# A gated mix of linear attention and a GLU on one core: the last stage's products, its addition of b, and how M is read

## The chip, the cores and the metric

The kernel runs on one core of a Trainium2 chip. The metric is the device time of one execution in microseconds (us); lower is better. TensorE multiplies into PSUM, VectorE and ScalarE work on SBUF and PSUM, and DMAs are issued here from two queues, SyncE's (SP) and GpSimd's (POOL).

## The reference

```python
H = 32; Dh = D // H                      # x: 2048 x 640
q, k, v = split_heads(x @ wqkv)
phi = lambda t: jnp.where(t > 0, t + 1, jnp.exp(t)) + 1e-6
kv = jnp.einsum("bhsd,bhse->bhde", phi(k), v)
z = jnp.einsum("bhsd->bhd", phi(k))
num = jnp.einsum("bhqd,bhde->bhqe", phi(q), kv)
den = jnp.einsum("bhqd,bhd->bhq", phi(q), z)[..., None] + 1e-6
a = merge_heads(num / den) @ wo
b = (_sigmoid(x @ w_gate) * (x @ w_up)) @ w_down     # F = 1536
g = _sigmoid((x * gate_w).sum(-1, keepdims=True))
return g * a + (1 - g) * b
```

Everything is fp32. The kernel uses that kv then wo is one matrix for all tokens: with M the 640 x 640 matrix of kv (32 blocks on a diagonal) times wo, and with P the phi(q) of a token scaled by g/den, g * a is P M. So the last stage is one product of 640 x 640 by 640 x 2048, to which (1 - g) * b is added.

## The kernel before

An fp32 product is made of three matmuls on halves: `split` (L245) takes the rounded half `hi` of an operand on ScalarE (`act`, L228) and the rest `lo` on VectorE (`vec2`, L232), and `mm3` (L215 to 218) multiplies hi by hi, hi by lo and lo by hi into the same PSUM tile. In the traces lines 216 to 218 are therefore nearly all of TensorE's work. A helper, `vec3`, stands at L236.

The tokens are four groups g of TG = 512, the 640 features KC = 5 rows u, k or o of 128. The output is kept transposed, so that one output tile is rows o of 128 features by 512 tokens of a group g: 5 x 4 = 20 tiles. A tile takes 5 terms k of 3 matmuls, 15 matmuls of 128x128 by 128x512. PSUM has four tags, `rot`, `dd`, `cc` and `ch`, of two buffers each.

Stages that matter here, in their order in time:
- Early on (DMAs of 163.6 to 188.4 us), `m_part` (L1227) writes M to `m_dram`, 120 rows at a time.
- The first pass of the GLU and of q, for groups 2 and 3 (`f_phase(1, ...)`), writes b of these groups to `b_dram`. At its step (3, 7) it calls `m_rows` (L1359): four DMAs on POOL's queue that copy `m_dram` to `mr_dram` with its rows permuted, so that a row of 128 partitions holds what phi(q)'s transposed rows need.
- The second pass, for groups 0 and 1 (`f_phase(0, ...)`), starts `queue_m` at its step (2, 7): a fifth u of `mr_dram` is loaded on SP's queue into the tile `mr`, split into the tile `mt`, written to `mp_dram` from POOL's queue, and then the next fifth is started. b of groups 0 and 1 is summed up in the SBUF tile `tb`; `last_down` (L1757) makes its last twenty sums, every second one by a DMA on POOL's queue that accumulates (`ds` to `tb`).
- Near the end of that pass the halves of M are loaded back from `mp_dram` (`load_m`, into tiles of the names `ws` and `wf`), and P of the groups from `p_dram` (`load_p`), where phi(q) had been put.

The names `ws`, `wu`, `wg` are tiles for the weights' forms in the GLU: each f of its blocks loads one of each on SP's queue (`load_form`, L901 to 903). The GLU's `Block` (L988) makes the four outputs of a 2 x 2 partition in seven products in place of eight, s1 to s7, with sums of operands and of outputs.

The last stage (the loop over `groups` = (2, 3, 0, 1)) makes the 20 tiles one after the other, here called units and numbered from 0. For each group it queues the scaling of its five b rows by 1 - g (`scale_b`, into the same tile `bl` or `tb`), first in the queue and from row 4 to row 0; then, for the next group, the scaling of P (`pq_scale`, L1882: plus EPS, times `fac`) and its split (`queue_pq`). After a unit `finish` (L1905) adds the PSUM tile to the scaled b row and sends it to the output. `load_b` loads 1 - g (`omg`) and b: for group 2 five DMAs, rows 4 to 0 (L1872), for group 3 two of three and two rows (L1876, L1877). The last unit is made in halves of 256 tokens.

The order of instructions on the engines is fixed by the program, not by a scheduler of the compiler. The class `Order` keeps a model of how far TensorE, ScalarE and VectorE have come, and queues of items with their costs. After each product `fill` issues the items whose end, by the model, is not more than some slack behind TensorE; an item can have a time before which it isn't taken (`ready`), `first=True` puts it before all others, `spare=True` behind them; `need(key)` issues all items up to that key at once. What stands in an engine's queue is done in that order, whatever arrives first. The lines that issue nothing but DMAs run where the Python runs them.

## Time and profile before

| | |
|---|---|
| median of three runs | 754.36 us (754.12 to 755.03) |
| the profiled execution's own time | 753.48 us |
| its span in the trace | 751.8 us |
| mean granted clock of TensorE | 0.999 |

The span is what the trace covers, from the first to the last instruction; the execution's own time has 1.68 us more around it. The busy time by stretches of the span:

```
us, PE busy (x) PEld busy (x) DVE busy (x) ACT busy (x) POOL busy (x), PEclk, DMA share, GB/s
330.00:520.00 190.00, 190.00 (x855) 157.83 (x855) 139.47 (x238) 83.49 (x148) 26.14 (x45) 1.00 0.69 249
520.00:606.00 86.00, 84.89 (x374) 69.94 (x373) 67.11 (x115) 28.84 (x51) 2.14 (x4) 1.00 0.66 243
606.00:679.00 73.00, 73.00 (x323) 60.39 (x323) 55.65 (x86) 20.37 (x36) 4.00 (x5) 1.00 0.54 187
679.00:751.80 72.80, 69.00 (x317) 56.95 (x315) 43.48 (x73) 9.72 (x16) 0.85 (x1) 0.99 0.51 172
```

PE is TensorE's matmuls, PEld its loads of weights, DVE VectorE, ACT ScalarE, POOL GpSimd; the DMA share is the mean busy share of the core's 16 DMA engines. The last stretch is the last stage. Matmuls are pipelined: the distance between the starts of two of them is their cost, and their own durations overlap. Some records of matmuls are missing from a trace (a few in a hundred), so that TensorE's line may show a hole that isn't one. A group of rows names its tiles as "out<-in"; the part in brackets is the idle time of the engine before the row, and what ended it.

### The profile page before, as it was taken

Reading aid. Unit: us, or ns where it says so; the run is one execution under the profiler, and the core shown is the slowest. Engines: PE = TensorE matmul, PEld = TensorE weight load, DVE = VectorE, ACT = ScalarE, POOL = GpSimd, SP = SyncE. Lnnn points to the kernel's source line nnn. Section 1 sums busy time; section 2 is a strip of 40 time slices with the busy share of each in tenths; the row PEclk is TensorE's granted clock in tenths of the full one; section 3 lists DMA queues with packets and bytes.
Section 4 is the critical chain, followed back from the end, with each engine's and each line's share of the span. In section 5 each row is a group of like instructions: output and inputs, shape, how many; then the busy total and the mean of one; then the engine's idle time right before and its main releaser. Section 6 shows DMA issues by size and latency. Waiting matters only on the chain.

```text
span 751.8 us, 10052 instructions
## 1 busy us (share of the span) xinstructions
PE 745.6 (99%) x3678; PEld 640.1 (85%) x3678; DVE 546.6 (73%) x964; ACT 316.9 (42%) x596; POOL 95.6 (13%) x153
## 2 busy tenths in 40 slices
PE   9999999999999999999999999999999999999998
PEld 8999999988888888888888888888788888888786
DVE  4877576867577768887878875576778876885854
ACT  5663537257555634343444354354223323222110
POOL 0210101012213422121211211000000000010000
PEclk9999999999999999999999999999999999999999
DMA  7563627686988888596675656967575656279333
GB/s 258 153 161 75 157 39 177 191 265 212 344 323 284 282 283 335 172 381 227 233 245 216 244 202 229 379 222 264 205 273 210 222 176 241 96 260 330 117 129 123
DMA packets 62758, 167.92 MB, mean 223 GB/s; under 512 B 9774, under 2 KB 23614, under 8 KB 59381
## 3 DMA queue, kind: packets, MB, share of 16 engines
q1 hardware_dynamic: 45941, 103.01, 40.9%
q0 software_dynamic: 16624, 64.10, 24.6%
q8 instruction: 29, 0.48, 0.3%
q10 hardware_dynamic: 144, 0.16, 0.1%
q14 instruction: 20, 0.16, 0.1%
HBM read 99.56 MB, written 62.78 MB: 216 GB/s over the span
## 4 chain that ended last, share of the span: by engine, by line
PE 93%; DMA 5%; DVE 1%; issue 0%; SPq 0%
PE ch L216 9%; PE ch L217 9%; PE ch L218 9%; PE dd L217 8%; PE dd L218 8%; PE dd L216 8%; PE rot L216 7%; PE rot L217 7%; PE rot L218 7%; PE cc L216 6%; PE cc L217 6%; PE cc L218 6%; DMA pl<-p_dram 2%; DMA ws<-wf 2%; DMA bl<-b_dram 1%; PE ch L1216 1%
## 5 line engine op out<-in xcount | busy, mean ns | idle before, releaser
L228 ACT ACTIVATE c<-ch 128x512 f32<-128x512 f32 x75 | 44.8, 597 | 161.4 <-PE ch L218 159.7
L232 DVE TENSOR_TENSOR hf<-c,hf 128x512 fp32r<-128x512 f32 x63 | 43.2, 688 | 30.2 <-ACT hf L228 29.7
L232 DVE TENSOR_TENSOR tb<-dd,tb 128x512 f32<-128x512 f32 x75 | 51.0, 687 | 12.1 <-PE dd L218 12.0
L232 DVE TENSOR_TENSOR c<-cc,c 128x512 f32<-128x512 f32 x50 | 34.4, 687 | 25.5 <-ACT c L228 19.5
L228 ACT ACTIVATE c<-c 128x512 f32<-128x512 f32 x48 | 30.2, 628 | 49.7 <-DVE c L232 49.6
L228 ACT ACTIVATE hf<-c 128x512 fp32r<-128x512 f32 x63 | 39.3, 625 | 18.4 <-DVE c L232 18.1
L232 DVE TENSOR_TENSOR tb<-rot,tb 128x512 f32<-128x512 f32 x59 | 40.0, 686 | 5.3 <-PE rot L218 5.2
L216 PE MATMUL ch<-xth,ws 128*128 128x512 f32 x100 | 39.0, 390 | 1.1 <-DMA ws<-wf 1.1
L218 PE MATMUL ch<-xth,ws 128*128 128x512 f32 x100 | 38.9, 389 | 0.0
L217 PE MATMUL ch<-xtl,ws 128*128 128x512 f32 x100 | 38.9, 389 | 0.0
L216 PE MATMUL dd<-xrh,wg 128*128 128x512 f32 x99 | 38.7, 391 | 0.0
L218 PE MATMUL dd<-xrh,wg 128*128 128x512 f32 x99 | 38.6, 390 | 0.0
L217 PE MATMUL dd<-xrl,wg 128*128 128x512 f32 x99 | 38.6, 390 | 0.0
L217 PE MATMUL rot<-pkl,xnh 128*128 128x320 f32 x102 | 31.5, 309 | 0.0
L218 PE MATMUL rot<-pkh,xnl 128*128 128x320 f32 x102 | 31.4, 308 | 0.0
L216 PE MATMUL rot<-pkh,xnh 128*128 128x320 f32 x102 | 31.4, 308 | 0.0
L232 DVE TENSOR_TENSOR c<-c,c 128x512 f32<-128x512 f32 x44 | 30.2, 686 | 1.3 <-ACT c L228 0.9
L216 PE MATMUL cc<-xbh,ws 128*128 128x512 f32 x75 | 29.2, 389 | 0.0
L217 PE MATMUL cc<-xbl,ws 128*128 128x512 f32 x75 | 29.2, 389 | 0.0
L218 PE MATMUL cc<-xbh,ws 128*128 128x512 f32 x75 | 29.2, 389 | 0.0
L216 PEld LDWEIGHTS ch<-xth,ws 128*128 128x128 f32 x100 | 18.8, 188 | 5.4 <-issue 1.5
L216 PE MATMUL dd<-hf,wd 128*128 128x512 f32 x60 | 23.3, 389 | 0.0
(482 smaller groups left out, 2286.4 us busy)
## 6 DMA issues: line engine op xcount, KB each, us to landing
wf<-ws POOLq DMA_DIRECT2D x12, 1152.0 KB, 6.5
ws<-wf SPq DMA_DIRECT2D x12, 1152.0 KB, 9.1
wst<-wst_f SPq DMA_DIRECT2D x12, 640.0 KB, 4.8
wf<-wg POOLq DMA_DIRECT2D x12, 640.0 KB, 5.3
wd<-wd POOLq DMA_DIRECT2D x12, 640.0 KB, 6.2
wg<-wf SPq DMA_DIRECT2D x12, 640.0 KB, 5.9
xst<-xt SPq DMA_DIRECT2D x10, 640.0 KB, 6.3
wf<-wd SPq DMA_DIRECT2D x10, 640.0 KB, 5.7
```

Of the source, the lines that this page charges most:

```text
L216: nc.tensor.matmul(out, l_hi, r_hi, start=first, stop=False, skip_group_check=True)
L217: nc.tensor.matmul(out, l_hi, r_lo, start=False, stop=False, skip_group_check=True)
L218: nc.tensor.matmul(out, l_lo, r_hi, start=False, stop=last, skip_group_check=True)
L228: nc.scalar.activation(out, src, fn, **kw)
L232: nc.vector.tensor_tensor(out, a, b, op=op)
L1216: nc.tensor.matmul(ps[:w, :w], v[:, m, :w], gt[:, m, c0:c0 + w], start=(m == 0), stop=(m == KC - 1))
```

## The change

There are three parts.

*The last stage.* P of group 1 is loaded before the stage's loop, right behind group 0's; b of groups 0 and 1 and the new loads of M behind the second unit. Groups 2 and 3 are made in units as before, and so are row 4 of group 0 and of group 1. Rows 0 to 3 of groups 0 and 1 are made in two blocks (`ABlock(0)`: rows 0 and 1, `ABlock(1)`: rows 2 and 3), each of which makes four tiles by seven products s1 to s7 of 2, 3, 2, 3, 2, 3 and 3 terms (s1, s2, s3, s4, s5, s7, s6 in the order of issue). For them `load_ms` reads two column pairs of M from `m_dram` again, by 16 DMAs on POOL's queue with pieces of 128 numbers, `queue_ms` makes the sums of M's blocks and splits them, and `queue_pt` the sums of P's blocks of groups 0 and 1.

*Gated b in PSUM.* The first three units scale b in SBUF and add it as before. For each later unit of groups 2 and 3, for row 4 of group 0, and for the s2 products, VectorE writes b times 1 - g into the PSUM tile before the products (`seed_b`), and the products are summed onto it; three units ahead, as an item that goes first. After such a unit ScalarE copies the tile to SBUF and the output is sent from there.

*M in permuted order.* `mr_dram` and its four DMAs are gone. `queue_m` reads the permuted rows straight from `m_dram`, by four DMAs of 32 rows on SP's queue for each fifth in place of one, and its item may be taken 14 us of the model after that, before 9.

```diff
-    mr_dram = dram.tile([P, KC, D], F32, name="mr_dram")
...
-    def m_rows():
+    def m_rows(dst, cols, queue, u=None):
 
         for d in range(4):
-            nc.gpsimd.dma_start(mr_dram[d * H:(d + 1) * H], m_dram.rearrange("(h u d) n -> d h u n", u=KC, d=4)[d])
+            m = m_dram.rearrange("(h u d) n -> d h u n", u=KC, d=4)[d]
+            queue.dma_start(dst[d * H:(d + 1) * H], m[:, u] if cols is None else m[:, :, cols])
 
     def queue_m(u=0):
 
         raw = down_pool[1].tile([P, D], F32, name="mr", tag="mr")
-        nc.sync.dma_start(raw, mr_dram[:, u])
-        at = max(order.pe, order.vec) + 9.0
+        m_rows(raw, None, nc.sync, u)
+        at = max(order.pe, order.vec) + 14.0
 
...
-        (3, 7): [m_rows],
...
-            PL[g] = []
+            PL[g], PL[g, "t"] = [], []
-                t = (x2_tile if n % 2 else h_tile)(dt=F32)
+                t = (x2_tile if n == 1 else h_tile)(dt=F32)
+                PL[g, "t"].append(t)
+        BL[g, "at"] = order.pe + 6.0
...
+    PT, MS, MR = {}, {}, {}
+    def load_ms(i):
+        if i == 0:
+            t = f32(down_pool[1].tile([P, 2, D], F32R, name="mt", tag="mt"))
+            raw = [t[:, j] for j in range(2)]
+        else:
+            raw = [down_pool[1].tile([P, D], F32, name=n, tag=n) for n in ("mr", "mv")]
+        for j in range(2):
+            c0 = (2 * i + j) * P
+            m_rows(raw[j].rearrange("p (k c) -> p k c", c=P), slice(c0, c0 + P), nc.gpsimd)
+        MR[i] = raw, order.pe + 9.0
+    def queue_ms(i):
+        raw, at = MR.pop(i)
+        w = 2 * P
+        g, v = raw
+        a11, a12, a21, a22 = g[:, :w], g[:, w:2 * w], v[:, :w], v[:, w:2 * w]
+        g5, v5 = g[:, 2 * w:], v[:, 2 * w:]
+        def sums(part):
+            if part == 0:
+                add(a22, a21, a22)
+                sub(a21, a11, a21)
+            else:
+                sub(a11, a22, a11)
+                sub(a12, a12, a11)
+                sub(g5, g5, v5)
+        def form(n, src):
+            if i not in MS:
+                t = ws_tile() if i == 0 else None
+                MS[i] = [t[:, c] for c in range(2)] if t is not None else \
+                    [wg_tile().rearrange("p a b -> p (a b)")[:, :9 * P] for _ in range(2)]
+            h, l = (t[:, n * w:n * w + width(src)] for t in MS[i])
+            split(h, l, src)
+        for part in range(2):
+            order.add(0, 2 * v_cost(w), lambda part=part: sums(part), None, lambda: at)
+        for n, t in enumerate((a22, a11, a21, a12, g5)):
+            order.add(a_cost(width(t)), v_cost(width(t)), lambda n=n, t=t: form(n, t), ("ms", i))
+    def queue_pt():
+        (b11, b21, _), (b12, b22, _) = PL[0, "t"], PL[1, "t"]
+        T = (b11, b22, b12, b21)
+        w = 2 * TG
+        def form(t):
+            if t == 1:
+                f = [[down_pool[2].tile([P, TG], F32R, name="pt", tag="c2", bufs=4) for _ in range(2)]
+                     for _ in range(2)]
+                PT[t] = f
+                for j in range(2):
+                    split(*f[j], T[t][:, j])
+                return
+            f = [x2_tile("pt", F32R) if t == 0 else x3_tile("pt", F32R) for _ in range(2)]
+            PT[t] = [[u[:, j] for u in f] for j in range(2)]
+            split(f[0][:, 0:2], f[1][:, 0:2], T[t])
+        def queue(t):
+            order.add(a_cost(w), v_cost(w), lambda: form(t), ("pt", t))
+        for a, b, c in ((b11, b12, b11), (b12, b22, b12), (b22, b22, b11), (b21, b21, b22)):
+            order.add(0, v_cost(w), lambda a=a, b=b, c=c: sub(a, b, c))
+        queue(1)
+        return queue
...
-    for gi, g in enumerate(groups):
-        for u in range(KC):
-            order.need(("pq", g, u))
-        for o in reversed(range(KC)):
-            order.add(0, v_cost(TG), lambda o=o: scale_b(g, o), ("b", g, o), first=True)
-        if 0 < gi < NG - 1:
-            nxt = groups[gi + 1]
-            queue_scale(nxt)
-            pq_tiles(nxt)
-            queue_pq(nxt)
-        for o in range(KC):
-            os_ = slice(o * P, (o + 1) * P)
-            cuts = (0, TG // 2, TG) if gi == NG - 1 and o == KC - 1 else (0, TG)
-            for c0, c1 in zip(cuts, cuts[1:]):
-                ps = ps_tile(("rot", "dd", "cc", "ch")[(o + gi) % 4])
-                prod(ps[:, c0:c1], [(MHL[k, 0][:, os_], MHL[k, 1][:, os_], PQ[g][k][0][:, c0:c1],
-                                     PQ[g][k][1][:, c0:c1]) for k in range(KC)], True)
-                order.need(("b", g, o))
-                finish(g, o, ps, c0, c1)
-            order.fill()
-        if gi == 1:
-            load_p(groups[3])
+    load_p(groups[3])
+    SEED = {}
+    def seed_b(g, o, tag):
+        SEED[g, o] = ps = ps_tile(tag)
+        vec2(ps, BL[g][o], OMG[g], OP.mult)
+    def queue_seed(g, o, tag, first=True):
+        order.add(0, v_cost(TG), lambda: seed_b(g, o, tag), ("b", g, o), lambda: BL[g, "at"], first=first)
+    def a_unit(g, o, cuts=(0, TG), tag="rot", seed=False):
+        os_ = slice(o * P, (o + 1) * P)
+        if seed:
+            order.need(("b", g, o))
+        for c0, c1 in zip(cuts, cuts[1:]):
+            ps = SEED.pop((g, o)) if seed else ps_tile(tag)
+            prod(ps[:, c0:c1], [(MHL[k, 0][:, os_], MHL[k, 1][:, os_], PQ[g][k][0][:, c0:c1],
+                                 PQ[g][k][1][:, c0:c1]) for k in range(KC)], not seed)
+            if seed:
+                dst = BL[g][o]
+                act(dst, ps, AF.Copy, "p")
+                nc.sync.dma_start(out_t[o * P:(o + 1) * P, g * TG:(g + 1) * TG], dst)
+                continue
+            order.need(("b", g, o))
+            finish(g, o, ps, c0, c1)
+    def queue_b_scale(g, os_):
+        for o in os_:
+            order.add(0, v_cost(TG), lambda o=o: scale_b(g, o), ("b", g, o), lambda: BL[g, "at"])
+    units = [(g, o) for g in groups[:2] for o in range(KC)] + [(groups[2], KC - 1)]
+    for n, (g, o) in enumerate(units[:-1]):
+        if o == 0:
+            for u in range(KC):
+                order.need(("pq", g, u))
+        if n == 0:
+            queue_b_scale(g, range(3))
+            queue_scale(groups[2])
+            for m in groups[2:]:
+                pq_tiles(m)
+        elif o == 0:
+            queue_scale(groups[3])
+            queue_pq(groups[3])
+            queue_pq(groups[2])
+            queue_t = queue_pt()
+            queue_ms(0)
+        a_unit(g, o, tag=("rot", "dd", "cc", "ch")[n % 4], seed=n > 2)
+        if n + 3 < len(units):
+            queue_seed(*units[n + 3], ("rot", "dd", "cc", "ch")[(n + 3) % 4])
+        if n == 8:
+            queue_seed(0, 0, "dd")
+        order.fill()
+        if n == 1:
             load_b(groups[2])
-        if gi == 2:
             load_b(groups[3])
+            load_ms(0)
+            load_ms(1)
+    class ABlock(Block):
+        def __init__(self, i):
+            self.o = (2 * i, 2 * i + 1)
+            self.i = i
...
+        def to_b(self, j, g, src, after="p"):
+            order.need(("b", g, self.o[j]))
+            add(BL[g][self.o[j]], src, BL[g][self.o[j]], after)
+        def s1(self):
+            self.ch, self.c11 = ps_tile("ch"), ct("c11")
+            prod(self.ch, [self.xa(0, j, j) for j in range(2)], True)
+            act(self.c11, self.ch, AF.Copy, "p")
+        def s2(self):
+            order.need(("b", 0, self.o[0]))
+            dd = SEED.pop((0, self.o[0]))
+            prod(dd, [self.xa(0, k, k) for k in range(2, KC)], False)
+            add(self.c11, dd, self.c11, "p")
+            self.out(0, 0, self.c11)
+        def s3(self):
+            order.need(("ms", self.i))
+            order.need(("pt", 1))
+            prod(self.ch, self.xt(2, 2, 1), False)
+            c12 = ct("c12")
+            act(c12, self.ch, AF.Copy, "p")
+            self.to_b(0, 1, c12, "a")
+        def s4(self):
+            order.need(("pt", 0))
+            self.cc = ps_tile("cc")
+            prod(self.cc, self.xt(2, 0, 0) + [self.xb(1, 2, 4)], True)
+            c22 = ct("c22")
+            act(c22, self.cc, AF.Copy, "p")
+            self.to_b(1, 1, c22, "a")
+        def s5(self):
+            order.need(("pt", 2))
+            prod(self.ch, self.xt(2, 4, 2), False)
+            c22 = ct("c22")
+            act(c22, self.ch, AF.Copy, "p")
+            self.to_b(1, 1, c22, "a")
+            self.out(1, 1, BL[1][self.o[1]])
+        def s6(self):
+            order.need(("pt", 3))
+            prod(self.ch, self.xt(1, 0, 3) + [self.xa(1, 2, 4)], False)
+            self.to_b(1, 0, self.ch)
+            self.out(1, 0, BL[0][self.o[1]])
+        def s7(self):
+            prod(self.cc, [self.xb(2, 6 + j, 2 + j) for j in range(2)] + [self.xb(2, 8, 4)], False)
+            self.to_b(0, 1, self.cc)
+            self.out(0, 1, BL[1][self.o[0]])
+    for u in range(KC):
+        order.need(("pq", 0, u))
+    queue_seed(0, 2, "dd")
+    queue_t(0)
+    queue_b_scale(1, (0, 1))
+    queue_t(2)
+    queue_t(3)
+    queue_ms(1)
+    queue_b_scale(0, (1,))
+    queue_b_scale(1, (2, 3))
+    queue_b_scale(0, (3,))
+    queue_b_scale(1, (4,))
+    a_unit(0, KC - 1, seed=True)
+    order.fill()
+    blocks = [ABlock(i) for i in range(2)]
+    for i, s in [(i, s) for i in range(2) for s in (1, 2)] + [(i, s) for i in range(2) for s in (3, 4, 5, 7, 6)]:
+        getattr(blocks[i], f"s{s}")()
+        order.fill()
+    a_unit(1, KC - 1, (0, TG // 2, TG))
```

`order.need(("pq", g, u))` and the like wait, in the model, for an item; the blocks' products use `ch`, `cc` and `dd` in PSUM, where s3, s5 and s6 sum onto what s1 left in `ch`, and s7 onto s4's `cc`.

More of the change, by code (lines that the diff above doesn't have):

```diff
@@ L1884, in pq_tiles @@
     def pq_tiles(g):
-        if groups.index(g) % 2 == 0:
+        if g == 1:
+            t = [x2_tile("pq", F32R) for _ in range(3)] + [h_tile() for _ in range(2)]
+            PQ[g, "t"] = [t[0:2], t[2:4]]
+        elif groups.index(g) % 2 == 0:
             t = [x2_tile("pq", F32R) for _ in range(5)]
-            PQ[g] = [(t[u // 2][:, u % 2], t[2 + u // 2][:, u % 2]) for u in range(4)] + [(t[4][:, 0], t[4][:, 1])]
+            PQ[g, "t"] = [t[0:3:2], t[1:4:2]]
         else:
@@ L1892, in pq_tiles @@
             PQ[g] = [tuple(t[:, u] for t in t2) for u in range(2)] + [tuple(t[:, u] for t in t3) for u in range(3)]
+            return
+        PQ[g] = [tuple(t[:, u % 2] for t in PQ[g, "t"][u // 2]) for u in range(4)] + [(t[4][:, 0], t[4][:, 1])]
     def queue_scale(g, lazy=False):
@@ L1956, in gated_mix_kernel, with w, xa, xb @@
             load_b(groups[2])
-        if gi == 2:
             load_b(groups[3])
+            load_ms(0)
[4 more added lines that the diff above has]
+            self.i = i
+        def w(self, i, c):
+            if i == 2:
+                return [t[:, c * P:(c + 1) * P] for t in MS[self.i]]
+            k, o = (c, self.o[0]) if i == 0 else (c + 2, self.o[1])
+            return [MHL[k, n][:, o * P:(o + 1) * P] for n in range(2)]
+        def xa(self, i, c, k):
+            return (*self.w(i, c), *PQ[0][k])
+        def xb(self, i, c, k):
+            return (*self.w(i, c), *PQ[1][k])
+        def xt(self, i, c, t):
+            return [(*self.w(i, c + j), *PT[t][j]) for j in range(2)]
+        def out(self, j, g, src):
+            o = self.o[j]
+            nc.sync.dma_start(out_t[o * P:(o + 1) * P, g * TG:(g + 1) * TG], src)
+        def to_b(self, j, g, src, after="p"):
[41 more added lines that the diff above has]
+            self.out(0, 1, BL[1][self.o[0]])
```

1 line of the change is left out of this document (added).

## The prediction

> **What bounds the kernel now.** I read the page first, for its shares and its chain. A step below is one TensorE instruction, a unit is one 128x512 output of the last stage (15 steps).
>
> ```profile
> span 751.8 us, 10052 instructions
> PE 745.6 (99%) x3678; PEld 640.1 (85%) x3678; DVE 546.6 (73%) x964; ACT 316.9 (42%) x596; POOL 95.6 (13%) x153
> ...
> PE 93%; DMA 5%; DVE 1%; issue 0%; SPq 0%
> ```
>
> TensorE sets the end, at 99%. Any saving must be counted in its steps, any cost in its pauses. So I went to TensorE's timeline, in the last stage and where the chain of waits leaves TensorE.
>
> ```profile
> 518.85 13.19 DMA ws<-wf
> ...
> 678.84 10.24 DMA bl<-b_dram
> 689.10 0.75 DVE bl L232 x2
> ```
> ```profile
> 530.67 0.39 PE L218 MATMUL cc<-xbh,ws 128*128 128x512 f32 x1
> 532.17 0.47 PE L216 MATMUL ch<-xth,ws 128*128 128x512 f32 x1 [1.11 <-DMA ws<-wf]
> ...
> 679.11 0.39 PE L216 MATMUL rot<-pq,ws 128*128 128x512 f32 x1
> ...
> 689.31 0.39 PE L216 MATMUL ch<-pq,ws 128*128 128x512 f32 x1
> ...
> 692.71 0.39 PE L216 MATMUL rot<-pq,ws 128*128 128x512 f32 x1
> ...
> 696.11 0.39 PE L216 MATMUL dd<-pq,ws 128*128 128x512 f32 x1
> ...
> 699.44 0.39 PE L216 MATMUL dd<-pq,wf 128*128 128x512 f32 x1
> ...
> 744.33 0.28 PE L216 MATMUL ch<-pq,ws 128*128 128x256 f32 x1
> ...
> 747.80 0.28 PE L218 MATMUL ch<-pq,wf 128*128 128x256 f32 x1
> ```
>
> The first columns are start and duration. From 689.31 to 692.71 lie the 15 steps of one unit: 3.40/15 = 0.2267 us a step. The stage runs from 679.11 to 747.80 almost without a pause. From 696.11 to 699.44 are 12 steps, 2.72 us at that pace, but 3.33 passed: a pause of 0.61, where the chain passes through VectorE, which began its work on the b rows only at 689.10, when the last of them landed. Elsewhere one pause stands out: 530.67 to 532.17 is 1.50 for one step, 1.27 lost, waiting for the load of `ws`.
>
> **The change, part by part.** *Steps.* Before, the stage has 20 units of 15 steps. After it has 12 such units, and eight outputs in two blocks of 2+3+2+3+2+3+3 = 18 terms, 54 steps each, so 108 for 120. Twelve steps fewer: 12 x 0.2267 = **-2.72**. The last unit stays in halves, and so does what follows it.
>
> *VectorE's order.* Before, scaling the five b rows of group 2 goes first in the queue and blocks it until 689.10.
>
> ```profile
> 679.61 0.69 DVE L236 SCALAR_TENSOR_TENSOR pl<-pl,fac 128x512 f32<-128x512 f32 x1
> 689.10 2.50 DVE L232 TENSOR_TENSOR bl<-bl,omg 128x512 f32<-128x512 f32 x4 [8.81 <-DMA bl<-b_dram]
> 691.52 0.68 DVE L232 TENSOR_TENSOR bl<-rot,bl 128x512 f32<-128x512 f32 x1
> ```
> ```profile
> DMA to landing us min/median/max: 3.8/8.4/17.1
> ```
>
> After, group 3 is scaled and split first, in those idle 8.81 us. Its loads (the second row: issued from 664.04 on, 17.1 at the latest) are in by about 682; four scalings and five differences remain, 9 x 0.60 = 5.4, done by 687.4. The pause at 696 to 699 had waited for these: **-0.61**.
>
> *The seeds.* From the fourth unit on, VectorE writes gated b into PSUM before the unit starts. Until now a unit needed b only when its 15 steps were over, and PSUM had two buffers for each tag. In the new order VectorE does: scale b 0, scale b 1, finish unit 0, seed unit 3. The first item waits for b row 0, which is loaded last and lands at 689.10; the others queue behind it though their data is there. Four operations of 0.60 (689.10 to 691.52 in the rows) end with the fourth's own 0.68 at 691.6. Unit 3 would have started at 689.31. So TensorE pauses 2.3, with 0.1 for starting again **+2.4**. A write into PSUM by VectorE stands in no row; from below it is an operation in SBUF (0.60), from above that plus half again, 0.3 more. I take 0.60, since a read from PSUM (691.52) costs no more than one from SBUF. The pause cannot be under 1.7 unless row 0 lands earlier.
>
> All later seeds then have that 2.4 us of grace. Unit 5's seed needs group 0's P (five scalings) and group 3's b; unit 8's needs group 1's P, which now loads right behind them.
>
> ```profile
> 686.89 0.37 SPq L1876 DMA_DIRECT2D bl<-b_dram  x1
> 687.74 0.37 SPq L1877 DMA_DIRECT2D bl<-b_dram  x1
> ```
> ```profile
> bl<-b_dram SPq DMA_DIRECT2D x1, 768.0 KB, 8.2
> bl<-b_dram SPq DMA_DIRECT2D x1, 512.0 KB, 8.7
> ```
> ```profile
> q1 hardware_dynamic: 1430, 2.74, 103.9%
> ```
>
> Group 3's b lands at 686.89 + 8.2 = 695.1 and 696.4. SP's queue is full then: 2.74 MB in 687 to 694, 0.39 MB a us, so the 1.31 MB of group 1's P follow at 699.8.
>
> *The new loads of M on POOL's queue.* Sixteen DMAs of 82 KB, in 512-byte pieces, wait for nothing late. They follow the last accumulation into tb.
>
> ```profile
> 680.25 0.85 POOL L1606 DMA_DIRECT2D tb<-ds  x1 [1.86 <-ACT ds L228]
> ```
> ```profile
> L1362 POOL DMA_DIRECT2D mr_dram<-m_dram x4: 971/980/994, 259.0 to 260.6; - x4
> ```
> ```profile
> q0 software_dynamic: 215, 0.39, 69.6%
> q1 hardware_dynamic: 218, 0.40, 40.2%
> ```
>
> At 0.98 us to issue one they go out from 681 to about 697, into a full machine; their pieces move once those of tb are through, from about 687, so row 0 of b is hardly touched. The two lower rows are 676 to 679, with tb's accumulations in flight: the queues took turn by turn (215 and 218 pieces) and SP's fell to 0.13 MB a us. What 512-byte pieces cost beside it no row shows. From below: only their bytes, 1.31/0.39 = 3.4 us in all, some 2 of them before group 3's b. From above: SP held at a third, as here, for the 12 us from 687. I take the bytes, as these loads do not accumulate. Then b of group 3 is in at 697.1, unit 5's seed at 697.8, needed at 696.11 + 2.4 = 698.5. Group 1's P is in at 703.2; its last scaling 0.6, five differences 3.0 and the seed 0.7 make 707.5, needed for unit 8 at 689.31 + 5 x 3.40 = 706.3, + 2.4 = 708.7. Both hold, **0**, with 0.7 and 1.2 to spare.
>
> The Trainium skill, "DMA: Bandwidth & Descriptors", section "Queues, rings and completion order", says that a DMA engine drains a whole packet of several descriptors from one queue before it turns to the next. The 215 to 218 agree with taking turns; whether 512-byte pieces travel bundled no row here shows. If they do, the sum would move to the upper bound, which is the first rival below.
>
> *Sums and forms for the blocks.* What VectorE does between the fourth seed and the second block's third product:
>
> ```profile
> L232 DVE TENSOR_TENSOR pq<-pl,pq 128x512 fp32r<-128x512 f32 x14 | 9.0, 688 | 0.9 <-ACT pq L228 0.9
> ...
> L232 DVE TENSOR_TENSOR wsum<-wst 128x256 f32<-128x256 f32 x24 | 9.1, 419 | 0.0
> ...
> L232 DVE TENSOR_TENSOR xbl<-xst,xbh 128x768 fp32r<-128x768 f32 x6 | 5.7, 952 | 0.9 <-ACT xbh L228 0.8
> ```
>
> 42 operations of 512 (0.60 from one to the next), 13 of 256 (0.36), 3 of 128 (0.2) and 7 of 1024 columns (688 + 2 x 264 = 1216 ns, 1.13 from one to the next): 25.2 + 4.7 + 0.6 + 7.9 = 38.4. TensorE takes from 691.7 to 734.6, 42.9. So VectorE just keeps up, and ScalarE, with 42% of the span, has room. Hidden by 4.5 us, **0**; without that cover each late us is a us of the time.
>
> *M read in permuted order.* Four row DMAs replace one for each fifth of M, mr_dram's copies go from POOL's queue (around 260, where nothing waits for them), and the due time moves by 5. In the instruction orders the second fifth's split moves from 517 to about 547, so the load behind it leaves SP's queue between `wu` and `ws`, and its write leaves POOL's.
>
> ```profile
> 518.27 0.32 SPq L1367 DMA_DIRECT2D mr<-mr_dram  x1
> ...
> 518.54 0.54 POOL L1375 DMA_DIRECT2D mp_dram<-mt  x1 [8.23 <-DVE mt L232]
> ```
> ```profile
> q0 software_dynamic: 134, 0.64, 38.4%
> ```
> ```profile
> mr<-mr_dram SPq DMA_DIRECT2D x1, 320.0 KB, 11.0
> ```
> ```profile
> q1 hardware_dynamic: 557, 2.50, 100.5%
> ```
>
> That write took 38.4% of the engines for 4 us (522 to 526), 1.5 us; the load, 0.33 MB at 0.42 MB a us (2.50 in 526 to 532), 0.8. `ws` landed at 532.04 and was needed at 530.90; 2.3 earlier is 529.7. The first fifth's write comes a little later and takes back up to 0.5. The pause at 530 goes, **-1.2** (bounds -1.27 and 0). The same work returns later, where the third fifth is split at 593.85 and its four loads stand before `ws` in SP's queue:
>
> ```profile
> 593.85 0.82 DVE L232 TENSOR_TENSOR mt<-mr,mt 128x640 fp32r<-128x640 f32 x1
> ```
> ```profile
> 594.68 0.32 SPq L903 DMA_DIRECT2D ws<-wf  x1
> ```
> ```profile
> ws<-wf SPq DMA_DIRECT2D x1, 1152.0 KB, 11.5
> ```
> ```profile
> 606.72 0.39 PE L216 MATMUL ch<-xth,ws 128*128 128x512 f32 x1
> ```
>
> Here `ws` lands at 594.68 + 11.5 = 606.2 and is needed at 606.72. With 0.8 of loads ahead it lands at 607.0; with the restart **+0.4** (0 if the queue has room, 1.9 if the four issues delay `ws` by their full time).
>
> Sum: -2.72 - 0.61 + 2.4 - 1.2 + 0.4 = -1.7. The profiled execution took 753.48 (751.8 and 1.68 around it), so 751.8 for it; the median of the runs, 754.36, is 0.88 higher and gives **752.7**.
>
> **Rivals.** *POOL's loads crowd out SP's* (the upper bound above). SP at a third for 12 us loses 8 us: group 1's P lands at 707.8, unit 8's seed is ready at 707.8 + 0.6 + 3.0 + 0.7 = 712.1, needed at 706.3, a pause of 5.8 in place of 2.4: 752.7 + 3.4 = 756.1, slower. It decides as soon as P lands after 706.1, where the pause passes 4.1 and all is given back. For it: the turns taken in 676 to 679. Against it: those pieces were four times as big and accumulated.
>
> *The early pause stays* because `ws` is late for its own bytes. Then -1.2 falls away and the later +0.4 stays: 753.9. For it: SP's queue has been full since 514 without POOL. Against it: 2.3 us of work leave, 1.2 are needed.
>
> *No pause before unit 3*, should row 0 of b land some 2.4 us earlier: 750.3. For it: the seed needs row 3 alone, loaded two before; against it: VectorE takes its work in order.
>
> *The clock drops during the long pause.* The 1.50 us at 530 did not lower it (0.227 us steps right after); half speed for 15 steps would cost 3.4: 756.1. The pause forecast is 1.6 times that one.
>
> **How the numbers follow.** Forecast 0.42, crowding 0.27, early pause stays 0.15, no pause 0.11, clock 0.05. Time 752.7; its own range, by the two bounds of the pauses at 606 and of the PSUM write, 752.0 to 754.3. The range must take in crowding and nearly all of the no-pause case: 750.5 to 757.0. Some 0.2% (1.5 us) is what can be told from no change: faster is below 752.85, slower above 755.87. Faster: 0.25 of the forecast's 0.42, the 0.11, 0.02 of others, 0.38. Slower: three quarters of crowding and clock, 0.24, and 0.04 for an unseen late form in VectorE's thin cover, 0.28. Same: 0.34.
>
> **What would show it.** Right: 12 fewer full steps; no pause near 530 and 697; one pause of 2.4 before the first `ch` unit of the stage that ends on VectorE's write of `ch` from `bl`; VectorE over 85% busy from there on. Wrong: a pause before units 5 or 8, or in the blocks, ended by a DMA or VectorE; `ws` waits of over 1 us near 605; a granted clock under 1.00 after the pause.

## The result, and the profile after

The changed kernel took 757.71 us in the median of six runs (756.87 to 759.01), the kernel before 754.14 (752.27 to 755.03) beside it: a ratio of 1.0055, with a 95% interval of 1.0039 to 1.0071. It is slower by half a per cent, where 752.7 was forecast and the range ended at 757.0.

The page of the changed kernel, its span, busy times and chain by engine:

```profile
span 757.0 us, 10179 instructions
PE 744.6 (98%) x3666; PEld 639.0 (84%) x3666; DVE 560.8 (74%) x989; ACT 332.8 (44%) x627; POOL 102.5 (14%) x165
...
PE 92%; DMA 6%; DVE 1%; SPq 0%; issue 0%; ACT 0%; DVEq 0%
```

TensorE has its 12 instructions less (3666 for 3678) and is done with them in 1.0 us less busy time, but the span is 5.2 us longer, and more of the chain is DMA. The chain of waits says where (start, duration, what):

```profile
679.46 13.53 DMA bl<-b_dram
693.08 0.75 DVE bl L232 x2
693.83 0.46 issue
694.29 0.68 DVE bl L232
694.97 0.62 DVE ch L232
695.63 0.79 PE ch L216
```

This is the place that the prediction named, VectorE's first item behind row 0 of b, with another number: the load takes 13.53 us where it took 10.24, and lands at 693.0 in place of 689.1. TensorE's timeline of the changed kernel (start, duration; the bracket is the idle time before):

```profile
530.77 0.39 PE L218 MATMUL cc<-xbh,ws 128*128 128x512 f32 x1
531.00 0.39 PE L216 MATMUL ch<-xth,ws 128*128 128x512 f32 x1
...
605.20 0.39 PE L218 MATMUL cc<-xbh,ws 128*128 128x512 f32 x1
606.03 0.47 PE L216 MATMUL ch<-xth,ws 128*128 128x512 f32 x1 [0.44 <-DMA ws<-wf]
...
678.53 0.39 PE L216 MATMUL rot<-pq,ws 128*128 128x512 f32 x1
...
688.50 0.39 PE L218 MATMUL cc<-pq,wf 128*128 128x512 f32 x1
695.63 0.79 PE L216 MATMUL ch<-pq,ws 128*128 128x512 f32 x1 [6.74 <-DVE ch L232]
...
701.66 0.39 PE L216 MATMUL rot<-pq,ws 128*128 128x512 f32 x1
...
705.07 0.39 PE L216 MATMUL dd<-pq,ws 128*128 128x512 f32 x1
...
753.42 0.28 PE L218 MATMUL rot<-hf,wf 128*128 128x256 f32 x1
```

The pause at 530 is gone (0.23 from step to step). At 605 one of 0.60 has come. The last stage begins at 678.53, 0.58 earlier than before. Then, from 688.50 to 695.63, 7.13 us pass for one step: 6.90 lost. Unit 3 lasts from 695.63 to 701.66, 6.03 in place of 3.40, and the stretches show why (after each engine's busy time and count, PEclk is the granted clock, then DMA share and GB/s):

```profile
679.00:688.50 9.50, 9.50 (x43) 7.87 (x42) 6.58 (x11) 3.45 (x6) 4.68 (x8) 1.00 1.09 294
688.50:695.60 7.10, 0.39 (x2) 0.00 (x0) 2.52 (x5) 0.00 (x0) 4.64 (x9) 0.90 1.06 280
695.60:701.00 5.40, 5.37 (x13) 4.21 (x14) 5.40 (x9) 0.00 (x0) 0.49 (x1) 0.50 1.05 283
701.00:753.00 52.00, 52.00 (x243) 43.56 (x242) 42.46 (x73) 21.99 (x41) 0.00 (x0) 1.00 0.37 137
```

TensorE's clock was granted at 0.50 behind the pause; from 701 to the end there is no pause at all. So the account of the two profiled executions is: 12 steps -2.72, the stutter at 696 to 699 -0.61, the pause before unit 3 +6.90, unit 3 at half clock +2.63, the pause at 530 -1.34 (1.27 and the slower step behind it), the one at 605 +0.68 (0.60 and 0.08): +5.5. Measured +5.2; what follows the last matmul took 3.6 us for 4.0 before. The small terms hold for these two executions alone: in a profile further down (the loads alone, in the kernel before), whose program is the same up to the stage, the pause at 530 was 0.40 in place of 1.27, and the stage began at 677.40 in place of 679.11.

Why row 0 came late stands in the queues. First 686 to 693 before, then the same stretch after (SP's queue q1, POOL's q0: packets, MB, share of 16 engines):

```profile
q1 hardware_dynamic: 1314, 2.49, 95.2%
q0 software_dynamic: 77, 0.12, 9.9%
```
```profile
q1 hardware_dynamic: 650, 1.25, 69.0%
q0 software_dynamic: 369, 0.61, 36.8%
...
bl<-b_dram SPq DMA_DIRECT2D x1, 768.0 KB, 14.5
```

The engines are full both times (105 and 106%). After, POOL's queue moved 0.49 MB more and SP's 1.24 MB less. Group 3's b needs 14.5 us from issue to landing, where it needed 8.2. In 687 to 691, with M's loads under way all along, the loss is plainer (before, then after):

```profile
q1 hardware_dynamic: 835, 1.58, 103.0%
q0 software_dynamic: 13, 0.01, 1.5%
```
```profile
q1 hardware_dynamic: 267, 0.51, 58.8%
q0 software_dynamic: 251, 0.43, 46.7%
```

SP's queue moved 0.13 MB a us, a third of its 0.40 before, and as much as beside the accumulations in the prediction's lines of 676 to 679 (0.40 MB in 3 us). Both queues together moved 0.94 MB in place of 1.59.

### The profile page after: what moved, and what is told of

Same layout as the page of the kernel before. It is cut to its first block, busy times and chain, and to the rows that moved or that the text cites. A ratio compares the mean times of both kernels' runs of the same rounds, so it can differ in the third digit from the quotient of the medians.

```text
span 757.0 us, 10179 instructions
## 1 busy us (share of the span) xinstructions
PE 744.6 (98%) x3666; PEld 639.0 (84%) x3666; DVE 560.8 (74%) x989; ACT 332.8 (44%) x627; POOL 102.5 (14%) x165
## 4 chain that ended last, share of the span: by engine, by line
PE 92%; DMA 6%; DVE 1%; SPq 0%; issue 0%; ACT 0%; DVEq 0%
PE ch L216 9%; PE ch L217 9%; PE ch L218 9%; PE dd L217 8%; PE dd L216 8%; PE dd L218 8%; PE rot L216 7%; PE rot L217 7%; PE rot L218 7%; PE cc L216 6%; PE cc L218 6%; PE cc L217 6%; DMA pl<-p_dram 2%; DMA bl<-b_dram 2%; DMA ws<-wf 1%; PE ch L1215 1%
## 5 line engine op out<-in xcount | busy, mean ns | idle before, releaser
L228 ACT ACTIVATE c<-ch 128x512 f32<-128x512 f32 x81 | 48.4, 597 | 172.5 <-PE ch L218 170.8
L232 DVE TENSOR_TENSOR tb<-rot,tb 128x512 f32<-128x512 f32 (+1 forms) x59 | 39.4, 676 | 8.2 <-PE rot L218 8.2
L216 PE MATMUL rot<-hf,wd 128*128 128x512 f32 x60 | 23.3, 389 | 0.0
```

What stands on the lines that cost most here:

```text
L216: nc.tensor.matmul(out, l_hi, r_hi, start=first, stop=False, skip_group_check=True)
L228: nc.scalar.activation(out, src, fn, **kw)
L232: nc.vector.tensor_tensor(out, a, b, op=op)
```

## The experiments

The ratios below are to the kernel before, run on the same chip in the same job, with a 95% interval; that kernel's median was 754.0, 753.2 and 753.8 in the three jobs.

**M's loads later, on SP's queue.**

```diff
-            m_rows(raw[j].rearrange("p (k c) -> p k c", c=P), slice(c0, c0 + P), nc.gpsimd)
+            m_rows(raw[j].rearrange("p (k c) -> p k c", c=P), slice(c0, c0 + P), nc.sync)
...
-            load_ms(0)
-            load_ms(1)
+        if n == 4:
+            load_ms(0)
+            load_ms(1)
```

> Edit: the sixteen new loads of M go out on SP's queue, behind the fourth seeded unit's turn (after unit 4), in place of POOL's queue after unit 1. Theory A (POOL's packets hold b of group 2 back): row 0 of b lands near 689.1 as in the kernel before, TensorE's pause before unit 3 shrinks from 6.9 to about 3.0 us (four VectorE operations of 0.60 after the landing), the clock does not fall after it, and 2.6 us of half-speed steps go: 757.7 - 3.9 - 2.6 = 751.2 us. Rival B (b is late for another reason, group 1's P or the order on SP's queue): row 0 still lands near 693 and the time stays at 757.7. Rival C: the late loads of M miss the blocks, a new pause ahead of the first s3 near 728, of 2 us or more.

754.19 us (ratio 1.0004, 0.9989 to 1.0019). Of the 3.6 us that the changed kernel lost to the one before, all came back, but not the expected 6.5. TensorE's timeline of this kernel:

```profile
688.08 0.39 PE L218 MATMUL cc<-pq,wf 128*128 128x512 f32 x1
692.03 0.80 PE L216 MATMUL ch<-pq,ws 128*128 128x512 f32 x1 [3.57 <-DVE ch L232]
692.62 0.63 PE L217 MATMUL ch<-pq,ws 128*128 128x512 f32 x1
693.05 0.63 PE L218 MATMUL ch<-pq,ws 128*128 128x512 f32 x1
```

VectorE took up b at 689.48, so theory A holds for the landing, and rival B falls; there was no pause later either, and C falls. But the pause was 3.72 us, and the steps after it took 0.43: the clock fell here too. In the ten timed runs the mean granted clock lay between 0.995 and 1.000, so the fall was not the same in all of them. Whether their pauses differed in length, or only in when they began, these runs do not show.

**b's rows from 0 to 4.**

```diff
-            for o in reversed(range(KC)):
+            for o in range(KC):
                 nc.sync.dma_start(BL[g][o], b_dram[:, o, g - 2])
```

> Edit: only the order in which group 2's b rows are loaded is turned round, row 0 first. The theory (VectorE's first item waits for row 0, which came last; POOL's packets stay as they are): row 0 lands near 686, row 3 near 692; VectorE is held by row 3 alone, for the seed of unit 3, and the pause shrinks from 6.9 to about 4.3 us. If a pause of 4.3 still drops the clock, 757.7 - 2.6 = 755.1; if not, 752.5. Rival (the order of the rows does not matter since the whole queue is late): 757.7.

759.00 us (1.0062, 1.0039 to 1.0085): no gain at all, though the pause before unit 3 shrank as expected, to 4.20. What is late next:

```profile
702.19 0.39 PE L218 MATMUL rot<-pq,wf 128*128 128x512 f32 x1
704.16 0.47 PE L216 MATMUL dd<-pq,ws 128*128 128x512 f32 x1 [1.58 <-DVE dd L232]
```

This is unit 5's first step, which waits for the write of group 3's b into `dd`; VectorE could begin that only at 703.31, when the b rows had landed. In the changed kernel unit 5 began at 705.07. There the slow clock had hidden this second wait.

**Both edits.**

> Edit: both edits together, M's new loads on SP's queue after unit 4 and b's rows from 0 to 4. Theory A with the order: row 3 lands near 688.4, the seed of unit 3 is written by 689.1, TensorE needs it at 688.7: a pause of 0.4 at most and no fall of the clock: 757.7 - 6.5 - 2.6 = 748.6. Rival: a seed or a form that was hidden by the long pause is late next (unit 5's seed waits for group 3's b, about 697 against 695.5; VectorE has 3 us less in the blocks): 750.5 to 752.

750.29 us (0.9940, 0.9922 to 0.9959): faster than both kernels. Against the changed kernel (1.0055) the later loads alone bring 0.5% (1.0004), the rows alone nothing (1.0062), and both together 1.1%: the first edit brings b in time and leaves VectorE waiting for its last row, the second takes that wait away, which is worth something only where group 3's b is in time as well. The time lies just under the rival's 750.5 to 752, but not by the rival's waits: the pause before unit 3 was 1.69 and not the expected 0.4, because VectorE had group 3's five splits to do first and took up b only at 687.24. That pause is this one, and no step is slow behind it:

```profile
687.87 0.39 PE L218 MATMUL cc<-pq,wf 128*128 128x512 f32 x1
689.79 0.50 PE L216 MATMUL ch<-pq,ws 128*128 128x512 f32 x1 [1.53 <-DVE ch L232]
690.12 0.39 PE L217 MATMUL ch<-pq,ws 128*128 128x512 f32 x1
```

**The pause filled with work.** In the changed kernel unit 2's products are made three times, outside the model, so that nothing else moves:

```diff
+            for _ in range(2 if (g, o) == units[2] else 0):
+                at = order.pe
+                prod(ps, [(MHL[k, 0][:, os_], MHL[k, 1][:, os_], *PQ[g][k]) for k in range(KC)], True)
+                order.pe = at
             prod(ps[:, c0:c1], ...
```

> Edit: the changed kernel, in which unit 2's fifteen steps are made three times (30 more steps, 6.8 us, same result), so that TensorE works through the pause before unit 3. Theory (the idle time itself drops the clock, and that costs 2.6 us on top): the pause of TensorE is under 0.3 us, the granted clock stays 1.00, unit 3 runs at 0.227 us a step: 757.7 - 2.6 = 755.1. Rival (the fall of the clock has another cause, or the pause's end moves by the added steps): 757.7 or more.

758.23 us (1.0056, 1.0036 to 1.0076). The clock stayed at 1.00, and nothing was won, because of unit 5 again:

```profile
703.40 0.39 PE L218 MATMUL rot<-pq,wf 128*128 128x512 f32 x1
704.76 0.47 PE L216 MATMUL dd<-pq,ws 128*128 128x512 f32 x1 [0.97 <-DVE dd L232]
```

So without the idle time the clock does not fall (theory), but in the changed kernel its 2.63 us cost next to nothing (rival): with them unit 5 starts at 705.07, without them at 704.76. What sets the end there is when group 3's b lands.

**The same with M's loads late**, where group 3's b is in time; 15 steps more:

> Edit: M's loads on SP's queue after unit 4, and unit 2's fifteen steps made twice (15 more steps, 3.4 us, same result), so that TensorE works through most of the pause of 3.72 before unit 3. Theory (idle time of 3.7 us lowers the clock for about 12 steps, and with b of group 3 on time nothing hides that): the pause is under 0.5 us, the clock stays 1.00, and the 12 x 0.2 + 0.36 = 2.7 us of slow steps are saved: 754.2 - 2.7 = 751.5. Rival (as with 30 added steps in the changed kernel, a later wait takes the gain): 754.2.

752.59 us (0.9991, 0.9982 to 1.0001). In the profile the pause and the slow steps are gone, and the span is 750.3 for 753.3 without the filling: 3.0, where 2.7 was expected. The medians differ by less, 0.13% by the ratios, whose intervals meet. The two profiles are also not quite the same case: here VectorE took up b at 687.62, where it was 689.48 without the filling, so that even without the added steps the pause would have been near 2 us. That the slow steps behind a pause of 3.72 us cost about 2.7 us is read from one profile; how much of it a typical run pays is not shown.

**The pause before unit 3 by another way: writes into PSUM from unit 6 on.** Units 3, 4 and 5 scale b in SBUF and add it as before, on top of both first edits.

```diff
-            queue_b_scale(g, range(3))
+            queue_b_scale(g, range(KC))
...
+            queue_b_scale(g, (0,))
             queue_scale(groups[3])
...
-        a_unit(g, o, tag=("rot", "dd", "cc", "ch")[n % 4], seed=n > 2)
-        if n + 3 < len(units):
+        a_unit(g, o, tag=("rot", "dd", "cc", "ch")[n % 4], seed=n > 5)
+        if 5 < n + 3 < len(units):
```

> Edit: the kernel with M's loads on SP's queue after unit 4 and b's rows from 0 to 4, in which the writes of gated b into PSUM begin with unit 6 in place of unit 3 (units 3, 4 and 5 scale b in SBUF and add it behind the products, as before). Theory (the 1.69 us left before unit 3 are the wait for VectorE's write, which stands behind group 3's five splits; a unit with an empty PSUM tile needs no VectorE before its start): that pause is gone and no other takes its place: 750.29 - 1.7 = 748.6. Rival (VectorE has three adds of 0.60 more, and TensorE reaches the blocks 1.7 earlier, so that a form is late there, before the first s3): 749.5 to 750.5.

752.95 us (0.9995, 0.9986 to 1.0005), worse than even the rival allowed. The pause before unit 3 is gone, but now TensorE waits for forms in the first block:

```profile
723.55 0.40 PE L216 MATMUL cc<-pt,ws 128*128 128x512 f32 x1
725.09 0.50 PE L217 MATMUL cc<-pt,ws 128*128 128x512 f32 x1 [1.14 <-DVE pt L232]
...
727.03 0.39 PE L216 MATMUL ch<-pt,ws 128*128 128x512 f32 x1
728.23 0.50 PE L217 MATMUL ch<-pt,ws 128*128 128x512 f32 x1 [0.81 <-DVE pt L232]
```

With those at 732 and 735 about 4 us are lost in the blocks. TensorE comes 1.7 earlier, VectorE has 1.8 more to do, and its order changes: these 3.5 us would still fit into the prediction's cover of 4.5, so the cover of single forms is thinner than that sum over the whole stretch. The writes into PSUM earn their place by the three adds that ScalarE takes over.

**No writes into PSUM but for s2**, M's loads on POOL's queue as in the changed kernel:

```diff
-            queue_b_scale(g, range(3))
+            queue_b_scale(g, range(KC))
...
+            queue_b_scale(g, range(KC))
             queue_scale(groups[3])
...
-        a_unit(g, o, tag=("rot", "dd", "cc", "ch")[n % 4], seed=n > 2)
-        if n + 3 < len(units):
-            queue_seed(*units[n + 3], ("rot", "dd", "cc", "ch")[(n + 3) % 4])
+        a_unit(g, o, tag=("rot", "dd", "cc", "ch")[n % 4])
...
+    queue_b_scale(0, (4,))
...
-    a_unit(0, KC - 1, seed=True)
+    a_unit(0, KC - 1, tag="cc")
```

> Edit: the changed kernel, with gated b written into PSUM for the two s2 products alone; all ten units of groups 2 and 3 and row 4 of group 0 scale b in SBUF and add it behind the products. M's loads stay on POOL's queue. Theory A (the writes into PSUM tie TensorE to b's landing, but POOL's packets make b and P late for VectorE all the same): no pause before units 3 and 5, the clock stays, TensorE reaches the first s3 of the blocks near 723, and VectorE, which starts on b at 693 and has 10 operations more, is late there by 5 to 8 us: 754 to 757. Theory B (the writes into PSUM alone are the loss): no pause anywhere: 757.7 - 6.9 - 2.6 = 748.2.

761.77 us (1.0114, 1.0099 to 1.0130). Theory B is far off, and A underrates it:

```profile
724.23 0.39 PE L218 MATMUL ch<-pq,wf 128*128 128x512 f32 x1
731.62 0.79 PE L216 MATMUL dd<-pq,wf 128*128 128x512 f32 x1 [7.01 <-DVE dd L232]
```

There is no pause before units 3 and 5. The late loads, with eight VectorE operations more (997 for 989, not the ten that were expected), end up in VectorE's queue and come out at the blocks, as 7.2 us and a slow clock, after 3.4 us in smaller pauses from 712.80 on. Without the writes the same lateness costs 4 us more.

**The loads alone, in the kernel before.** Nothing reads what they load.

```diff
+            if gi == 0 and o == 1:
+                t = f32(down_pool[1].tile([P, 2, D], F32R, name="mt", tag="mt"))
+                raw = [t[:, j] for j in range(2)]
+                raw += [down_pool[1].tile([P, D], F32, name=n, tag=n) for n in ("mr", "mv")]
+                for j in range(4):
+                    for d in range(4):
+                        m = m_dram.rearrange("(h u d) n -> d h u n", u=KC, d=4)[d]
+                        nc.gpsimd.dma_start(raw[j][d * H:(d + 1) * H].rearrange("p (k c) -> p k c", c=P),
+                                            m[:, :, j * P:(j + 1) * P])
```

> Edit: the kernel before, with the sixteen loads of M added on POOL's queue at the changed kernel's place, into tiles that nothing reads. Theory (the loads hold back SP's loads, and even units that don't need b before their start wait, as VectorE splits group 3's P behind the scaling of b): row 0 of b lands near 693, VectorE scales it 4 us later, group 3's splits are 4 us late for unit 5, where TensorE pauses 4 to 4.5 us in place of 0.6: 757.5 to 758.5. Rival (only the writes into PSUM tie TensorE to b): 754.

758.78 us (1.0072, 1.0046 to 1.0097). Sixteen transfers of 1.31 MB in all, which no instruction waits for, cost 5 us, more than the whole change lost:

```profile
694.40 0.39 PE L216 MATMUL dd<-pq,ws 128*128 128x512 f32 x1
698.87 0.79 PE L217 MATMUL dd<-pq,ws 128*128 128x512 f32 x1 [4.08 <-DVE pq L232]
```

The pause has the expected place and size (4.24); that the clock falls behind it too was not in the sum. So the writes into PSUM are not needed for the loss.

**The same loads on the same queue, 38 us earlier**, with b's rows from 0 to 4:

```diff
-        (FC - 1, 7): [lambda: load_m(1)],
+        (FC - 1, 7): [lambda: load_m(1), lambda: load_ms(0), lambda: load_ms(1)],
...
-            load_ms(0)
-            load_ms(1)
```

> Edit: M's sixteen new loads stay on POOL's queue with the same pieces, but go out some 38 us earlier, behind the write of 1 - g at 642, when SP's queue carries little; b's rows from 0 to 4. Theory (it is the moment at which POOL's packets meet SP's loads of b and P that costs, not the queue or the pieces): b lands as it does with M's loads late on SP's queue (row 3 near 688.4, group 3's b near 695 to 696.5), TensorE pauses 1.7 us before unit 3, the clock stays, and the time is that kernel's: 750.0 to 750.5 against 754.0 of the kernel before. Rival (loads in 642 to 655 push the loads for the stage, P of group 2 and M's halves, back): a pause at the start of the stage, near 678, and 751 or more.

750.50 us (0.9956, 0.9942 to 0.9971). Neither POOL's queue nor the pieces of 512 bytes do the harm by themselves; it takes the moment. (The same loads at the old moment on SP's queue were not tried.) That the time fell into the expected 750.0 to 750.5 is in part luck, for the pause before unit 3 was 0.57 and not 1.7: the stage began at 678.92, where it was 677.89 in the kernel with both first edits. The rival did not cause that; TensorE was 1.0 behind that kernel already at 606, before these loads go out. Where they go out now there was room (641 to 655 in the changed kernel, then here):

```profile
641.00:655.00 14.00, 14.00 (x64) 11.56 (x63) 11.90 (x19) 3.49 (x7) 0.55 (x1) 1.00 0.38 136
```
```profile
641.00:655.00 14.00, 14.00 (x63) 11.57 (x63) 11.91 (x19) 3.76 (x7) 9.68 (x17) 1.00 0.70 215
```

**Group 3's splits behind the scaling of b**, on top of that:

```diff
-    queue_pq(groups[1])
...
             queue_b_scale(g, range(3))
+            queue_pq(groups[1])
```

> Edit: the kernel with M's loads early on POOL's queue and b's rows from 0 to 4, in which group 3's five splits are queued behind the scaling of b in place of ahead of it. Theory (the 1.7 us left before unit 3 are VectorE's five splits of 0.60 ahead of b): the seed of unit 3 is written by about 689.0, right after row 3's landing, the pause shrinks from 1.7 to 0.9, and the splits are still in time for unit 5 near 695: 0.8 less than without this edit. Rival (the seed of unit 4 or a form in the blocks is late instead): no gain or a loss of up to 1.

749.44 us (0.9947, 0.9931 to 0.9963), 0.5% faster than the kernel before. Unit 3 starts 0.24 after the step before it (688.08 to 688.32): the pause is all but gone, 0.57 in the kernel without this edit. The intervals of the three fast versions, this one, the one with both first edits and the one above, overlap, so that what this edit alone is worth is not shown.

**The same bytes in one piece of 2560 for each partition.**

```diff
-            c0 = (2 * i + j) * P
-            m_rows(raw[j].rearrange("p (k c) -> p k c", c=P), slice(c0, c0 + P), nc.gpsimd)
+            m_rows(raw[j], None, nc.gpsimd, 2 * i + j)
```

> Edit: the changed kernel, in which the sixteen loads take as many bytes of M in one piece of 2560 bytes for each partition (whole rows) in place of five of 512; so the sums of M in the two blocks are made of other numbers. Theory (the queues take turns packet by packet, and POOL's packets were already bundles of eight such pieces, so that its share of the engines is the same): row 0 of b lands near 693, group 3's b near 703, and the time is the changed kernel's, 757.7. Rival (it is the small pieces that hold SP back): row 0 lands by 691 and group 3's b by 699, and the time falls to 754 or less.

756.93 us (1.0045, 1.0029 to 1.0061): nearly the changed kernel's time. In 686 to 693 SP's queue now moved this much:

```profile
q1 hardware_dynamic: 835, 1.58, 72.9%
q0 software_dynamic: 249, 0.60, 31.8%
```

0.33 of the 1.24 MB come back, and the pause before unit 3 is 5.89 for 6.90. So the small pieces are about a quarter of the matter, and neither expectation was met in full. The other three quarters stay with large pieces. What of them is due to a second queue as such, and what to transfers that write only 32 partitions each, no run here separates.

**The new way to read M, alone**, in the kernel before (the diff's parts for `m_rows`, `queue_m` and `mr_dram`):

> Edit: the kernel before, with the changed way of reading M alone (four row DMAs for a fifth, straight from m_dram, due time 14). Theory: the pause of 1.34 at 530 goes and one of 0.7 comes at 605, as in the changed kernel, and nothing else moves: 754.1 - 0.6 = 753.5. Rival (the row DMAs cost more than that on SP's queue, and part of the changed kernel's loss lies here): 754.1 or more.

752.89 us (0.9999, 0.9989 to 1.0008): no difference, and so no part of the changed kernel's loss. The pause at 530 is gone, and 1.40 us have come back at 605:

```profile
605.45 0.39 PE L218 MATMUL cc<-xbh,ws 128*128 128x512 f32 x1
607.08 0.47 PE L216 MATMUL ch<-xth,ws 128*128 128x512 f32 x1 [1.24 <-DMA ws<-wf]
```

In the kernels with this path the second pause was between 0.1 and 1.40: `ws` lands about when it is needed, and the third fifth's loads stand before it.

## Why the prediction was wrong

- **The steps, -2.72:** right. The blocks ran without a pause in the changed kernel, and in the three fast versions too.
- **The stutter at 696, -0.61:** right; unit 5 has no step there that is longer than the others.
- **Reading M, -1.2 and +0.4:** right in place, -1.34 and +0.68 in the two profiles; alone, the two cancel. The size of the first is partly luck, since the pause at 530 was 0.40 in another profile of the same instructions.
- **VectorE's order before unit 3, +2.4:** the mechanism was right (scale, scale, finish, write, behind row 0 of b), and the number was wrong, since it stood on row 0's landing at 689.1. The step that failed is the sentence on the new loads of M, that "their pieces move once those of tb are through, from about 687, so row 0 of b is hardly touched". They did move from about 686, and row 0 landed at 693.0. SP's queue still had rows of b to bring then, and beside M's loads it moved them at a third of its rate.
- **"I take the bytes, as these loads do not accumulate":** the second step that failed, in the same place. By bytes SP would have lost 0.49 MB in 686 to 693, and it lost 1.24. Group 3's b, forecast for 697.1, landed at 703.2 and let VectorE write unit 5's PSUM at 703.29. The upper bound, SP at a third for 12 us and 8 us lost, came close: 703.2 is 8 us behind the 695.1 without M's loads. The reasons against it, that the pieces beside which SP fell to a third were four times as big and accumulated, did not count: SP fell to the same 0.13 MB a us. The kernel before with the loads alone shows that they cause the loss by themselves, and the same loads 38 us earlier that they cost nothing that can be seen where the queues have room.
- **The rival of crowding** had the right mechanism, but the wrong unit and a price too low, 756.1, because it was worked out for group 1's P at unit 8 alone, where the changed kernel has no pause. The same 8 us applied to group 3's b at unit 5 would have given 695.1 + 8 + 0.7 = 703.8, against the 696.11 at which unit 5 began before: a pause of 7.7 in place of 2.4, 758.0. One rate was used for one load, and every load behind it in the queue should have had it.
- **What is won ahead of a wait** was counted twice. With M's loads late, so that POOL's queue does not hold b back, the pause before unit 3 was still 3.72 and not 2.4. TensorE was ready for unit 3 at 688.31, 1.0 before the 689.31 of the sum, and VectorE took up b at 689.48, 0.4 after the 689.1. The sum credits the 0.8 that reading M was to win, and then takes the pause from the old 689.31, though row 0 did not land earlier for it.
- **The clock,** a rival at 0.05, came true beside crowding and not in place of it. It fell in every profile with a pause of 3.72 us or more. Here it cost next to nothing, since unit 5 was late anyway (filled pause: 758.23 for 757.71).
- **VectorE's cover of 4.5 us in the blocks:** enough in the changed kernel, where TensorE came late itself, but not shown to be that large: 3.5 us less of it left 4 us of pauses in the blocks.

## What to carry to other kernels

A transfer that nothing waits for is not free: on full DMA engines, price it by how much it slows the queue that it shares them with, measured from a stretch where two queues met, and apply that rate to every load still to land. The sixteen loads cost 5 us at 687 and nothing that shows at 645; look for an idle stretch before another queue. Time that is won ahead of a wait for a DMA is lost in that wait if the landing does not move with it. And when a wait is shortened, name what is late next: turning b's rows round brought nothing while group 3's b was late, and 0.6% once it wasn't.

## What the runs showed of the hardware

- *Two queues on full engines cost more than their bytes.* Packets in 686 to 693, counted in the trace's records (mean time of one; POOL's are the accumulations into tb before, M's loads after):

```
before  SP 2048 bytes x1218, 0.087 us   POOL 2048 bytes x61, 0.178 us
after   SP 2048 bytes x 608, 0.126 us   POOL 4096 bytes x111, 0.259 us; 1024 bytes x112, 0.063 us
```

  The pieces of 512 bytes travelled eight and two to a packet, and SP's own packets of 2048 bytes took 45% longer beside them. The Trainium skill, "DMA: Bandwidth & Descriptors", section "Queues, rings and completion order", says that an engine takes turns between queues packet by packet and drains a whole packet first. The bundles fit that, but strict turns do not follow: in 687 to 691, with both queues at work, 249 data packets of SP's went beside 170 of POOL's, and 325 beside 78 where M's pieces were 2560 bytes. Whether a packet of the trace is a packet in that sense is not shown, and why SP's packets become slower is open.
- *The granted clock falls to 0.50 after idle time, for 6.83 us, and the length of the pause alone does not decide when.* A pause of 2.34 (in the kernel without the writes, at 712.80) and those of 1.69 and less left 0.227 us a step; 3.72, 4.20, 4.24, 5.89, 6.90 and 7.16 were followed by 7 to 12 slow steps, most of 0.43. In all six of these traces the clock's record stands at 0.50 for 6.83 us, in the changed kernel from 694.18 to 701.01 and with M's loads late from 690.55 to 697.37; the slow steps are what is left of that time when TensorE goes on. The fall came 5.45 us into the pause of 6.90 that began at 688.73, but 2.24 us into that of 3.72 that began at 688.31. The record's whole stretches at 0.50 and 1.00 are multiples of 3.413 us (6.83 is two, the 689.49 before the changed kernel's fall 202, the 686.08 before the other's 201), so that it matters how a pause lies to this grid; no run here tests that by itself. The Trainium skill, "TensorE: Matmul & The Clock Gate", section "What's actually happening", gives a free-running window of 3.4 us and lets the clock fall after an idle one. The grid agrees with it; the fall after 2.24 us shows that less than a whole idle window can be enough.
- *A write of VectorE into PSUM is no dearer than one into SBUF:* 0.60 us from one operation to the next in both (694.29, 694.89 and 695.49 in the changed kernel's VectorE timeline).
